# Splitting the list of the halves ahead, loading small slots before the last scatters, and putting the loop of small slots in a branch, in an attention-plus-mixture-of-experts kernel

## The chip, the cores and the metric

One core of a Trainium2 chip runs the whole kernel as one program. The metric is the device time of one execution in microseconds, taken as the median of three runs. The engines are called PE (TensorE, matmuls), DVE (VectorE), ACT (ScalarE), POOL (GpSimd, which also issues the indirect DMAs, that is gathers and scatters by a list of rows) and SP (SyncE, which issues most loads).

## What is computed

Four batches of channel attention are followed by a mixture of experts with one expert for each token (a token is a row of 256 floats; there are 20,224 of them, 8 experts, 1024 hidden features):

```python
qn, kn = q / norm(q, axis=1), k / norm(k, axis=1)
s = kn.transpose(0, 2, 1) @ qn / tau            # 256 x 256 for each batch
x = (v @ softmax(s)).reshape(20224, 256)
out = x
do = x @ w_skip > 0                             # the tokens that are computed
e = argmax(x[do] @ w_gate)                      # one expert each
out[do] += softmax(x[do] @ w_gate)[e] * (relu(x[do] @ w1[e]) @ w2[e])
```

The inputs are drawn from a fixed seed. In them one expert has nearly all of the computed tokens: 9,902, of which 2,461 lie in the first four chunks (below) and 4,941 in the first eight; each of the other seven has at most 54.

## The kernel before

**Phases.** A batch is four chunks of 1,280 tokens, so there are 16 chunks. Step A of a chunk loads q and k and adds to the scores (PE, L731). When a batch's four A steps are done, its softmax runs. Step B of a chunk multiplies v with the softmax (L804 to L806, in two parts of higher and lower bits), ACT copies the rows to `xo` (L811) and stores them to `out`, `logits` and `route` pick an expert for each token, and ten POOL scatters for each chunk (L886) write (token, gate) to the list `lst` in DRAM, where every expert has its own stretch.

**Halves ahead.** While the later B steps run, the kernel already computes experts for the expert with most tokens: nine halves of 512 tokens (H0 to H8), taken from its list as it stands after eight chunks (D0 = 8). After four chunks (D1 = 4) `Large.ahead` picks that expert, so that its weights can be gathered (`w1r`, `w2r`; two POOL gathers). After eight chunks it looks whether the expert has 512·9 + 128 + 64 tokens by then; if so, one POOL load brings their list, `lN`, from `lst`; if not, the address points past the lists, at empty entries. A half then takes four gathers (L213, through `gather_ahead`) into one of three buffers `xg`, eight PE transposes into `pt` (L286), the split of the transposed rows into `xH` (ACT, L288) and `xL` (DVE, L290), two layers of matmuls (L320 to L322 into the buffer `px`, then L342 and L343) and four scatters back to `out` (L218, through `put_ahead`). The weights are split too: `w1H` on ACT (L313), `w1L` on DVE (L315), four pieces each. Before a batch's softmax can be used, the sums of squares `n` (L718, L720) go through PE and DVE (`nrm`, L744), and v is split into `vH` (ACT) and `vL` (DVE, L693).

**Tails.** Steps T0 to T3 compute the first 64 tokens of every expert, two experts at a time (buffers `tg`, weights `v1r` and `v2r`); T4 computes 128 more of the busiest.

**Loops.** What is left of the lists is cut into slots: `large.loop()` (a hardware loop at L447, 1,024 tokens a round; its code for a slot holds L320 x32) and `small.loop()` (L596, slots of 128 tokens). With these inputs the first runs five rounds and the second none. Ahead of the small loop stand its first loads (`load_rows`: five small lists through SP, two gathers into `yg`; `load_weights`: three weight gathers into `v1r` and `v2r`), two transposes and `keep_warm(4)` (four PE products of `ones` that nobody reads). The small loop ends with one scatter, of `yo`.

**What sets the order.** `ORDER` is a string written by hand ("... B9 B2 B3 A10 B4 ... A15 B9 H0 B10 ... H8 T2 T3"); it gives every PE step a nominal time. A list scheduler, `Plan`, gives each task an engine, a cost, the tasks that it depends on and a due time, and writes each engine's instructions in the order that comes out. An engine executes its instructions in that order, so that a waiting instruction holds up those behind it. `now` is the nominal time at the end of the string. At the start of `large.loop()` all engines meet (L447). `beside` and `apart` tell the framework that two groups of transfers don't touch the same data.

## Time and profile before

| | us |
|---|---|
| median of three runs | 800.12 (799.33 to 801.84) |
| the profiled execution | 797.65 |
| its span in the trace | 796.0 |
| PE busy in it | 761.3 (96%) |
| DVE busy | 472.4 (59%) |
| POOL busy | 389.5 (49%) |
| ACT busy | 334.2 (42%) |
| share of the 16 DMA engines: loads, indirect DMAs, stores | 27.3%, 10.5%, 8.2% |

PE is busy nearly all of the time, so a change that doesn't take work from PE can gain at most where PE stands still or runs slowly. The view that finds such places cuts the span into stretches and gives each engine's busy time, and the TensorE clock that was granted (1.00 is the upper of its two levels, 2.4 GHz; 0.50 the lower, 1.2 GHz). The timeline of one engine then lists its instructions with start, duration and, in brackets, the idle time just ahead of an instruction and what ended it.

### The profile page before, as it was taken

To read this page: it belongs to the slowest core of one execution; us is meant where nothing else is said; L and a number is where in the kernel's file an instruction comes from. 1 tells how busy PE (TensorE), PEld (TensorE's weight loads), DVE (VectorE), ACT (ScalarE), POOL (GpSimd) and SP (SyncE) were. 2 spreads that over 40 slices of the span, in tenths; PEclk is the share of its full clock that TensorE was granted. 3 is DMA by queue.
4 is the path that set the end of the run, shared out by engine and by line. 5 is a ranking of instruction groups with operands and counts; after the bars stand their busy time and mean duration, and the time that the engine had idled before them with its cause. 6 is when DMAs were issued, how large, how long until landed. Compare 5 with 4: busy or idle time off the path is not lost. (4 is left out here: it accounts for less than half of the span.)

```text
span 796.0 us, 12212 instructions
## 1 busy us (share of the span) xinstructions
PE 761.3 (96%) x4268; PEld 656.4 (82%) x4268; DVE 472.4 (59%) x968; ACT 334.2 (42%) x515; POOL 389.5 (49%) x411
## 2 busy tenths in 40 slices
PE   6999999999979999999999999996999999999994
PEld 5889998999968989889888886754888888888883
DVE  4809958898978773664547442513555564656652
ACT  5519748668756442432332223112233332423330
POOL 3000277778758777657667523124434344253532
PEclk9999999999998999999999999998999999999997
DMA  8979979899552471641246313453211111111100
GB/s 318 399 251 330 372 247 298 310 396 384 172 184 103 130 219 34 232 147 34 93 163 224 141 41 103 182 217 134 94 46 47 46 47 45 41 47 46 46 20 29
DMA packets 55218, 127.50 MB, mean 160 GB/s; under 512 B 14556, under 2 KB 34792, under 8 KB 52480
## 3 DMA queue, kind: packets, MB, share of 16 engines
q1 hardware_dynamic: 18000, 79.75, 27.3%
q0 software_dynamic: 15936, 26.39, 10.5%
q10 hardware_dynamic: 21232, 20.72, 8.2%
q8 instruction: 27, 0.44, 0.2%
q14 instruction: 23, 0.19, 0.1%
HBM read 109.03 MB, written 31.93 MB: 177 GB/s over the span
## 5 line engine op out<-in xcount | busy, mean ns | idle before, releaser
L886 POOL DMA_INDIRECT lst<-pay,r_posi x160 | 179.5, 1122 | 141.6 <-DVE r_posi L883 93.3
L731 PE MATMUL s<-qt,kt 128*128 128x256 f32 x640 | 150.2, 386 | 6.2 <-DMA kt<-in_k 6.2
L218 POOL DMA_INDIRECT out<-xg,lc x78 | 81.0, 1038 | 142.7 <-DVE xg L349 124.1
L731 PEld LDWEIGHTS s<-qt,kt 128*128 128x128 f32 x640 | 120.1, 193 | 21.0 <-issue 6.2
L342 PE MATMUL po<-w2s,hH 128*128 128x512 f32 x320 | 113.7, 398 | 0.4 <-issue 0.4
L342 PE MATMUL px<-w2s,hH 128*128 128x512 f32 x288 | 102.6, 399 | 0.0
L804 PE MATMUL px<-aH,vH 128*128 128x266 f32 x320 | 99.8, 312 | 0.2 <-ACT xo L811 0.2
L213 POOL DMA_INDIRECT xg<-out,lc x80 | 82.0, 1025 | 31.3 <-issue 18.3
L325 ACT ACTIVATE hH<-ph 128x512 fp32r<-128x512 f32 x80 | 47.9, 599 | 110.4 <-PE ph L322 109.9
L805 PE MATMUL px<-aL,vH 128*128 128x266 f32 x320 | 92.7, 290 | 0.0
L806 PE MATMUL px<-aH,vL 128*128 128x266 f32 x320 | 92.4, 289 | 0.0
L343 PE MATMUL po<-w2s,hL 128*128 128x256 f32 x320 | 89.5, 280 | 0.0
L326 DVE SCALAR_TENSOR_TENSOR hL<-ph,hH 128x512 fp32r<-128x512 f32 x80 | 55.4, 692 | 47.4 <-ACT hH L325 46.4
L343 PE MATMUL px<-w2s,hL 128*128 128x256 f32 x288 | 80.6, 280 | 0.0
L811 ACT COPY xo<-px 128x532 f32<-128x532 f32 x80 | 47.8, 603 | 74.0 <-PE px L806 71.4
L342 PEld LDWEIGHTS po<-w2s,hH 128*128 128x128 f32 x320 | 60.0, 188 | 14.5 <-issue 0.8
L320 PE MATMUL ph<-xH,w1H 128*128 128x512 f32 x160 | 63.4, 396 | 7.0 <-PEq L447 7.0
L416 DVE SCALAR_TENSOR_TENSOR hL<-px,hH 128x512 fp32r<-128x512 f32 x72 | 46.4, 685 | 39.7 <-ACT hH L414 39.6
L342 PEld LDWEIGHTS px<-w2s,hH 128*128 128x128 f32 x288 | 54.0, 188 | 12.7 <-issue 0.8
L321 PE MATMUL ph<-xL,w1H 128*128 128x512 f32 x160 | 63.2, 395 | 0.0
L322 PE MATMUL ph<-xH,w1L 128*128 128x512 f32 x160 | 63.1, 394 | 0.0
L804 PEld LDWEIGHTS px<-aH,vH 128*128 128x128 f32 x320 | 61.5, 192 | 1.7 <-ACT xo L811 0.6
(216 smaller groups left out, 1428.6 us busy)
## 6 DMA issues: line engine op xcount, KB each, us to landing
vf<-in_vt SPq DMA_DIRECT2D x32, 640.0 KB, 7.2
qt<-in_q SPq DMA_DIRECT2D x31, 640.0 KB, 6.5
kt<-in_k SPq DMA_DIRECT2D x31, 640.0 KB, 6.5
out<-xo ACTq DMA_DIRECT2D x12, 1280.0 KB, 7.6
v1r<-in_w SPq DMA_DIRECT2D x8, 1024.0 KB, 6.2
v2r<-in_w SPq DMA_DIRECT2D x8, 1024.0 KB, 4.9
lst<-pay,r_posi POOLq DMA_INDIRECT x160, 4.1
out<-xo ACTq DMA_DIRECT2D x4, 640.0 KB, 6.1
```

Source lines behind the costliest of these rows:

```text
L213: apart(G.indirect_dma_start(out=to, out_offset=None, in_=out[0:n, :], in_offset=IndirectOffsetOnAxis(ap=ls[:, 0:1], axis=0), bounds_check ...
L218: i = (G.indirect_dma_start(out=out, out_offset=IndirectOffsetOnAxis(ap=ls[:, 0:1], axis=0), in_=src, in_offset=None, bounds_check=NTOK - ...
L320: T.matmul(ph, self.w1H[:, fs], self.xH[:, kb, :], start=(kb == 0), stop=False)
L321: T.matmul(ph, self.w1H[:, fs], self.xL[:, kb, :], start=False, stop=False)
L322: T.matmul(ph, self.w1L[:, fs], self.xH[:, kb, :], start=False, stop=(kb == 1))
L342: T.matmul(po, self.hH[:, f, ts], self.w2s[:, f, :, :], start=(f == 0), stop=False, skip_group_check=True)
L343: T.matmul(po[:, :C], self.hL[:, f, ts], self.w2s[:, f, 0, :], start=False, stop=(f == NFB - 1), skip_group_check=True)
L731: T.matmul(sums[b][:, cb, :], kt[:, j % JH, cb * P : (cb + 1) * P], qt[:, j % JH, :], start=(ch == 0 and j == 0 and cb == 0), stop=(ch == ...
L804: T.matmul(px[:, i, :NA], vH[:, kb, js], aH[:, kb, :], start=(kb == 0), stop=False)
L805: T.matmul(px[:, i, :NA], vH[:, kb, js], aL[:, kb, :], start=False, stop=False)
L806: T.matmul(px[:, i, :NA], vL[:, kb, js], aH[:, kb, :], start=False, stop=(kb == 1))
L886: i = G.indirect_dma_start(out=lst, out_offset=IndirectOffsetOnAxis(ap=posi[:, t : t + 1], axis=0), in_=pay[:, t0 + t, :], in_offset=None, ...
```

## The change

1. **The list in two parts.** `lA` (16 columns: halves 0 to 3) is loaded after four chunks, `lB` (21 columns: halves 4 to 8 and T4) after eight. The choice is made twice: at four chunks (at least 512·4 + 64 = 2,112 tokens of one expert, else an address past the lists), and at eight as before. Halves 0 to 3 gather only from the rows of the first four chunks.
2. **Small slots' first loads earlier.** `load_rows` comes in three pieces: the five small lists as soon as the tables are there, the two gathers at a due time of `now` − 6, and the weights (`load_weights`) at `now` − 4 after T2's second layer; before, they had `now` + 6 and `now` + 10, after every scatter of the tails. `keep_warm(12)` stands ahead of `large.loop()`.
3. **The small loop in a branch.** Its transposes, `keep_warm(4)` and the loop are in the `Else` of `tc.If(n < 1)`.

```diff
+KA = 4
-            self.lN = rows([P, 4 * K0 + 1, 2], I32, name="lN")
+            self.lA = rows([P, 4 * KA, 2], I32, name="lA")
+            self.lB = rows([P, 4 * (K0 - KA) + 1, 2], I32, name="lB")
+            self.lN = rows([P, 8, 2], I32, name="lN")
...
+            def address(i, first):
+                V.tensor_scalar(adf, e0, float(CAP), float(E * CAP + first), ALU.mult, ALU.add)
+                V.tensor_scalar(ads[i], adf, float(E * CAP), None, ALU.min)
+
+            V.tensor_reduce(many, cnt4, AX.X, ALU.max)
+            V.scalar_tensor_tensor(most, cnt4, many, iota8, ALU.is_ge, ALU.mult)
+            V.tensor_reduce(top, most, AX.X, ALU.min)
+            V.scalar_tensor_tensor(e0, many, 512.0 * KA + T0, top, ALU.is_ge, ALU.mult)
+            address(0, T0)
...
+            apart(load_list(ads[0], 0, self.lA, 4 * KA, G), "lists A", "of the first chunks alone")
+            yield
...
+            address(1, T0 + 512 * KA)
...
-            beside(load_list(ad0, 0, self.lN, 4 * K0 + 1, G), "first lists", "later lists")
+            apart(load_list(ads[1], 0, self.lB, 4 * (K0 - KA) + 1, G), "lists B", "of the first chunks alone")
...
         def gather_ahead(self, x, t):
             h = self.AHEAD[x]
+            l, y, d = (self.lA, x, D1) if x < KA else (self.lB, x - KA, D0)
             if t == 0:
-                G.tensor_copy(self.lc[h], self.lN[:, 4 * x : 4 * x + 4, :])
-            self.gather_tile(h, t, D0 // NCH * N + D0 % NCH * P * J)
+                G.tensor_copy(self.lc[h], l[:, 4 * y : 4 * y + 4, :])
+            self.gather_tile(h, t, d // NCH * N + d % NCH * P * J)
...
-            if d >= D0:
-                beside(i, "later lists", "first lists")
+            for of, l in ((D1, "lists A"), (D0, "lists B")):
+                if d >= of:
+                    apart(i, l, "of the first chunks alone")
...
-    pick = add("V", 1.5, lambda: next(rows), [based[D1 - 1]])
-    look = add("V", 1.3, lambda: early.append(next(rows)), [based[D0 - 1], pick])
-    lst0 = add("D", 1.0, None, [add("G", 1.05, lambda: next(rows), [look, listed0, stored[D0 - 1]])])
+    pick = add("V", 2.3, lambda: next(rows), [based[D1 - 1]])
+    lstA = add("D", 1.0, None, [add("G", 1.2, lambda: next(rows), [pick, listed4, stored[D1 - 1]])])
+    look = add("V", 1.4, lambda: early.append(next(rows)), [based[D0 - 1], lstA])
+    lstB = add("D", 1.0, None, [add("G", 1.2, lambda: next(rows), [look, listed0, stored[D0 - 1]])])
...
-    sm = add("G", 3.0, lambda: smalls[0].load_rows(slots[0][1], slots[1][1]), [tabled, so, in_order["sc"], *stored.values(), n2, pt], due=now + 6)
-    add("G", 3.2, lambda: smalls[0].load_weights(), [sm, n3], due=now + 10)
...
+    sm = add("V", 1.2, small_rows, [tabled, so, in_order["sc"], *stored.values(), n1])
+    sm = add("D", 1.5, None, [sm])
+    sm = add("G", 3.1, small_rows, [sm, n2], due=now - 6)
+    add("G", 4.0, lambda: smalls[0].load_weights(), [sm, n3, tails[2]], due=now - 4)
...
+        keep_warm(12)
         large.loop()
-        smalls[0].transposed(0)
-        keep_warm(4)
-        smalls[0].loop()
+        with tc.If(smalls[0].n < 1, preferred_fallthrough_block=False) as none_left:
+            pass
+        with none_left.Else():
+            smalls[0].transposed(0)
+            keep_warm(4)
+            smalls[0].loop()
```

**POOL ahead of H0.** POOL's instructions around the first list, before (`lst` are the list's scatters, `xg` the gathers of a half, `lc` the half's own copy of its list):

```order
L225 DMA w1r<-in_w,wc 128x2048
L225 DMA w2r<-in_w,wd 128x2048
L886 DMA lst<-pay,r_posi 168960x2 x40
L230 TENSOR_LOAD ad_2156
L230 ISA x2
L231 ISA
L231 DMA lN<-lst 128x74
L402 COPY lc_152<-lN 128x8
L213 DMA xg_144<-out,lc_152 128x256 x4
L402 COPY lc_153<-lN 128x8
L213 DMA xg_145<-out,lc_153 128x256 x2
```

The same place now:

```order
L226 DMA w1r<-in_w,wc 128x2048
L898 DMA lst<-pay,r_posi 168960x2 x10
L231 TENSOR_LOAD ads_1372
L231 ISA x2
L232 ISA
L232 DMA lA<-lst 128x32
L226 DMA w2r<-in_w,wd 128x2048
L898 DMA lst<-pay,r_posi 168960x2 x20
L412 COPY lc_154<-lA 128x8
L214 DMA xg_144<-out,lc_154 128x256 x4
L412 COPY lc_155<-lA 128x8
L214 DMA xg_145<-out,lc_155 128x256 x4
```

The first list now stands behind 10 scatters that follow `w1r`, not 40, and the gathers of halves 0 and 1 behind 30; the ten scatters of chunk 7 come after ten gathers.

**DVE ahead of H0.** The last instructions of DVE before H0's first matmul (`lg`, `r_mx` and `r_d` are routing), before and now:

```order
L827 COPY lg<-xo 128x100
L744 TENSOR_SCALAR nrm<-n 128x260
L838 TENSOR_REDUCE r_mx<-lg 128x10
L840 TENSOR_TENSOR r_d<-lg,r_mx 128x80
L693 TENSOR_TENSOR vL<-vf,vH 128x1280
L290 TENSOR_TENSOR xL<-pt,xH 128x512
L315 TENSOR_TENSOR w1L<-w1r,w1H 128x512 x4
L290 TENSOR_TENSOR xL<-pt,xH 128x512
```

```order
L756 TENSOR_SCALAR nrm<-n 128x260
L705 TENSOR_TENSOR vL<-vf,vH 128x1280
L318 TENSOR_TENSOR w1L<-w1r,w1H 128x512
L293 TENSOR_TENSOR xL<-pt,xH 128x512
L318 TENSOR_TENSOR w1L<-w1r,w1H 128x512 x3
L293 TENSOR_TENSOR xL<-pt,xH 128x512
L839 COPY lg<-xo 128x100
```

One of the four splits of w1 now stands ahead of the first `xL`, and the routing of the next chunk behind the second. On PE the same products of B stand between the last A and H0 (48 of them), with `n` and the two groups of four transposes spread between them.

**POOL at the entry of the large loop.** Before, and now (`tg` are the tails' scatters; L447, now L457, is the loop):

```order
L218 DMA out<-xg_146,lc_154 20224x256 x4
L218 DMA out<-tg_4566,tl 20224x256
L218 DMA out<-tg_4562,tl 20224x256
L218 DMA out<-tg_4563,tl 20224x256
L218 DMA out<-tg_4564,tl 20224x256
L218 DMA out<-tg_4565,tl 20224x256
L584 MEMSET mc_4558 128x2
L213 DMA yg_4540<-out,mc_4557 128x256
L213 DMA yg_4541<-out,mN_4554 128x256
L225 DMA v1r_4532<-in_w,vc_4549 128x2048
L225 DMA v1r_4533<-in_w,vc_4550 128x2048
L225 DMA v2r_4536<-in_w,vd_4551 128x2048
```

```order
L214 DMA yg_4558<-out,mc_4575 128x256
L214 DMA yg_4559<-out,mN_4572 128x256
L226 DMA w2r<-in_w,wd 128x2048
L219 DMA out<-xg_146,lc_156 20224x256 x4
L219 DMA out<-tg_4584,tl 20224x256
L219 DMA out<-tg_4580,tl 20224x256
L219 DMA out<-tg_4581,tl 20224x256
L226 DMA v1r_4550<-in_w,vc_4567 128x2048
L226 DMA v1r_4551<-in_w,vc_4568 128x2048
L226 DMA v2r_4554<-in_w,vd_4569 128x2048
L219 DMA out<-tg_4582,tl 20224x256
L219 DMA out<-tg_4583,tl 20224x256
```

The two `yg` gathers moved ahead of the scatters of H8, the three weight gathers ahead of the scatters of T2 and T3; behind T3's scatter there is now only the loop.

## Rows read from the trace of the kernel before

**Rows 1.** Busy time by stretch: start and end in us; length; then busy us and count of PE, PEld, DVE, ACT and POOL; the granted clock of PE (1.00 is the upper level); share of the DMA engines; GB/s. The stretches are cut where PE stands still: the last A step ends at 229.34, H0's first matmul starts at 245.54, the last matmul ahead of the large loop ends at 543.22, the clock is back at 554.93, the last matmul of the large loop ends at 783.14.

```profile
6.18:229.34 223.16, 222.68 (x1290) 203.56 (x1291) 171.96 (x322) 150.13 (x183) 101.91 (x87) 1.00 0.88 316
229.34:245.54 16.20, 10.19 (x63) 9.51 (x62) 8.36 (x19) 7.86 (x14) 12.65 (x13) 0.79 0.52 171
245.54:543.22 297.68, 294.58 (x1710) 244.05 (x1708) 156.87 (x382) 95.84 (x176) 167.74 (x169) 1.00 0.40 134
543.22:554.93 11.71, 4.75 (x11) 3.79 (x12) 3.31 (x13) 1.69 (x3) 8.16 (x9) 0.71 0.46 161
...
783.14:796.00 12.86, 1.31 (x11) 1.14 (x10) 0.97 (x2) 0.68 (x2) 2.91 (x3) 0.65 0.10 25
```

**Rows 2.** Timeline of PE, from the last A step (it ends at 229.34) to H0: start us, duration us, instruction, and in brackets the idle time ahead of it and what ended it.

```profile
228.99 0.47 PE L804 MATMUL px<-aH,vH 128*128 128x266 f32 x1
...
232.15 0.59 PE L718 MATMUL n<-sqq,ones 128*128 128x256 f32 x2
...
240.06 0.47 PE L286 MATMUL pt<-ident,xg 128*128 128x128 f32 x1 [3.94 <-DMA xg<-out,lc]
...
245.54 0.39 PE L320 MATMUL px<-xH,w1H 128*128 128x512 f32 x1
```

**Rows 3.** Timeline of POOL from 163 us to 231 us: the first and the last of the 40 scatters of chunks 4 to 7, the list and the first gather of half 0.

```profile
163.18 1.10 POOL L886 DMA_INDIRECT lst<-pay,r_posi  x1 [0.30 <-issue]
...
221.38 1.78 POOL L886 DMA_INDIRECT lst<-pay,r_posi  x1 [0.31 <-issue]
224.92 0.59 POOL L231 DMA_DIRECT2D lN<-lst  x1 [1.76 <-DMA lst<-pay,r_posi]
228.44 0.19 POOL L402 COPY lc<-lN 128x8 int32<-128x8 int32 x1 [2.93 <-DMA lN<-lst]
229.56 1.41 POOL L213 DMA_INDIRECT xg<-out,lc  x1 [0.94 <-POOL lc L402]
```

**Rows 4.** Timelines of DVE and ACT in the same place.

```profile
233.12 0.43 DVE L744 TENSOR_SCALAR nrm<-n 128x260 f32<-128x260 f32 x1
...
233.88 1.53 DVE L693 TENSOR_TENSOR vL<-vf,vH 128x1280 fp32r<-128x1280 f32 x1
241.19 0.69 DVE L290 TENSOR_TENSOR xL<-pt,xH 128x512 fp32r<-128x512 f32 x1 [5.78 <-ACT xH L288]
241.79 2.49 DVE L315 TENSOR_TENSOR w1L<-w1r,w1H 128x512 fp32r<-128x512 f32 x4
...
240.57 0.59 ACT L288 CAST xH<-pt 128x512 fp32r<-128x512 f32 x1 [5.21 <-PE pt L286]
```

**Rows 5.** Timeline of POOL around 330 us (the last gather of half 4) and of PE at 357 us (half 4's transposes).

```profile
331.56 1.00 POOL L213 DMA_INDIRECT xg<-out,lc  x1 [0.30 <-PE px L806]
...
357.02 0.60 PE L286 MATMUL pt<-ident,xg 128*128 128x128 f32 x4
```

**Rows 6.** DMA issues by tile: count and median us from issue to landing.

```profile
xg<-out,lc POOLq DMA_INDIRECT x80, 2.8
out<-xg,lc POOLq DMA_INDIRECT x78, 2.4
v1r<-in_w,vc POOLq DMA_INDIRECT x2, 7.5
```

**Rows 7.** Timeline of PE at the entry of the large loop.

```profile
538.96 3.67 PE L560 MATMUL px<-v2r,thT 128*64 128x256 f32 x32 [0.24 <-ACT thT L552]
542.56 0.66 PE L286 MATMUL pt<-ident,xg 128*128 128x128 f32 x4
550.18 0.76 PE L320 MATMUL ph<-xH,w1H 128*128 128x512 f32 x1 [6.96 <-PEq L447]
...
554.98 0.40 PE L322 MATMUL ph<-xH,w1L 128*128 128x512 f32 x1
555.23 0.40 PE L320 MATMUL ph<-xH,w1H 128*128 128x512 f32 x1
555.46 0.39 PE L321 MATMUL ph<-xL,w1H 128*128 128x512 f32 x1
```

**Rows 8.** Timelines of POOL and of SP's queue ahead of that entry (the row of SP is the two loads of T3's second weights).

```profile
543.44 0.97 POOL L218 DMA_INDIRECT out<-tg,tl  x1 [4.37 <-DVE tg L562]
...
549.14 1.00 POOL L225 DMA_INDIRECT v1r<-in_w,vc  x1 [0.30 <-POOLq L447]
...
528.20 0.80 SPq L514 DMA_DIRECT2D v2r<-in_w  x2
```

**Rows 9.** The instructions of line 447 (the large loop): count, min/median/max ns, first and last start in us. The first start is when that engine's queue reaches the meeting point.

```profile
L447 POOLq EVENT_SEMAPHORE  x82: 17/43/43, 547.6 to 784.2; - x82
...
L447 DVEq EVENT_SEMAPHORE  x68: 21/21/21, 543.9 to 784.3; - x68
```

**Rows 10.** Timeline of all engines from the last matmul of the large loop to the end.

```profile
784.80 1.06 PE L1248 MATMUL m<-ones 128*128 128x128 f32 x8
...
786.43 0.97 POOL L218 DMA_INDIRECT out<-xg,lc  x1 [0.30 <-POOLq L596]
792.31 0.97 POOL L218 DMA_INDIRECT out<-yo,mc  x1 [4.90 <-PEq L1298]
```

**Rows 11.** The jumps of line 596 (the small loop, which runs no round): count, min/median/max ns, first and last start.

```profile
L596 ACTq COMPARE_BRANCH  x2: 34/36/38, 786.4 to 786.5; - x2
L596 PEldq COMPARE_BRANCH  x2: 69/2068/4067, 786.5 to 786.7; - x2
```

More of the change, by code (lines that the diff above doesn't have):

```diff
@@ L370, in ahead @@
         def ahead(self, cnt0, cnt4):
-            top = tab.tile([P, 1], F32, name="top")
-            V.tensor_reduce(top, cnt4, AX.X, ALU.max)
-            V.scalar_tensor_tensor(cnt4, cnt4, top, iota8, ALU.is_ge, ALU.mult)
-            V.tensor_reduce(top, cnt4, AX.X, ALU.min)
-            most = tab.tile([P, E], F32, name="most")
-            V.tensor_scalar(most, iota8, top, None, ALU.is_equal)
+            top, many, e0, adf = (tab.tile([P, 1], F32, name=n) for n in ("top", "many", "e0", "adf"))
+            ads = [tab.tile([P, 1], I32, name=f"ads{i}") for i in range(2)]
+            most, start = (tab.tile([P, E], F32, name=n) for n in ("most", "start"))
+            def address(i, first):
[6 more added lines that the diff above has]
+            address(0, T0)
+            V.tensor_scalar(start, iota8, e0, 512.0 * KA, ALU.is_equal, ALU.mult)
+            V.tensor_scalar(start, start, float(T0), None, ALU.add)
+            V.tensor_scalar(most, iota8, e0, None, ALU.is_equal)
             V.tensor_scalar(top, top, float(E), None, ALU.add)
@@ L1075, in attn_moe @@
             listed0 = add("D", 0.06, None, [in_order["sc"]])
+        if d == D1 - 1:
+            listed4 = add("D", 0.06, None, [in_order["sc"]])
         if d == NC - 1:
@@ L1128, in attn_moe @@
         for i in range(4):
-            gt = then("gat", add("G", 1.31 if i else 1.9, lambda x=x, i=i: large.gather_ahead(x, i), [lst0, puts.get(x - 3)]))
+            gt = then("gat", add("G", 1.31 if i else 1.9, lambda x=x, i=i: large.gather_ahead(x, i), [lstA if x < KA else lstB, puts.get(x - 3)]))
             gd = add("D", 0.36, None, [gt])
@@ L1199, in attn_moe @@
         tw = [None] * 4 if p == NP else [then("tw", add("D", 2.95, small("tail_weights", p, w, u), [so, (firsts, tails)[w].get(p - 2)], nominal["T", p, 2 * w] - 1)) for w in range(2) for u in range(2)]
-        tg = then("tg", add("G", 1.3, small("tail_gather", p), [tld, listed0 if p == NP else None]))
+        tg = then("tg", add("G", 1.3, small("tail_gather", p), [tld, lstB if p == NP else None]))
         tgd = add("D", 0.3, None, [tg])
@@ L1235, in attn_moe, with small_rows @@
     n3.deps.append(tails[NP])
[L1236 to L1237 removed]
+    def small_rows():
+        if not early[2:]:
+            early.append(smalls[0].load_rows(slots[0][1], slots[1][1]))
+        next(early[2])
+    sm = add("V", 1.2, small_rows, [tabled, so, in_order["sc"], *stored.values(), n1])
+    sm = add("D", 1.5, None, [sm])
+    sm = add("G", 3.1, small_rows, [sm, n2], due=now - 6)
+    add("G", 4.0, lambda: smalls[0].load_weights(), [sm, n3, tails[2]], due=now - 4)
     def counts():
```

17 lines of the change are left out of this document (6 added, 11 removed).

## Prediction

> **What bounds the kernel now.** I read the busy time by stretch first [rows 1]. PE works through the A steps without a gap (222.68 us busy of 223.16) and nearly so from H0 to the large loop (294.58 of 297.68); the change takes no matmul out of these. What it can win lies in three stretches where PE stands still and then, or meanwhile, runs at a lower granted clock: 16.20 us ahead of H0 (10.19 busy, clock 0.79), 11.71 us at the entry of the large loop (4.75 busy, clock 0.71), and 12.86 us from the last matmul to the end (1.31 busy). Each of the three parts of the change aims at one of them, so I read the timelines of the engines there.
>
> Ahead of H0, PE is ready to transpose and waits for gathers: the last wait is 3.94 us, for xg [rows 2]. Behind that wait stands POOL: it issues the 40 scatters of chunks 4 to 7 from 163.18 to 223.16, waits 1.76 us for the last one to land, loads the list, waits 2.93 us for that, and starts the first gather at 229.56, after the last A step [rows 3]. POOL's place in its own queue is the bound.
>
> At the loop's entry PE's last work starts at 542.56 and takes 0.66, so it ends at 543.22; the first product of the loop starts at 550.18, released by the meeting of the engines [rows 7]. DVE reaches the meeting at 543.9, POOL only at 547.6 [rows 9]: after T3's scatter (543.44, 0.97 us) it still issues the first loads of the small slots, the last but one at 549.14 [rows 8]. After the pause the products start too far apart until about 555: 11 of them take 4.80 us (550.18 to 554.98), at 0.23 us each afterwards they would take 2.5 [rows 7].
>
> At the end, POOL's scatters of the last slot start by 786.43, but one more, of yo, from a loop that runs no round, starts only at 792.31 [rows 10]. It waits for PE's jump past that loop's code: 4.07 us for PE, 0.04 for ACT [rows 11].
>
> **Part 1, the list.** Forty scatters took 59.98 us, 1.50 each [rows 3]. The first list now stands behind ten of them and the gathers of halves 0 and 1 behind twenty more, one list load (0.59 and up to 2 of waiting, which the next weight gather covers) and w2r. So the scatters of chunk 6 end near 163 + 30·1.5 = 208; eight gathers at 1.31 (1.00 and 0.31 between) end near 219, and land 2.8 us later by the median [rows 6]. Even at three times that landing they are there before PE ends the A steps at 229.34. The wait for xg goes.
>
> What is late next? PE has the same work left after the last A: 48 products of B from 228.99 on (24 of them took 3.16 us, so 6.32), n and its pair (232.15 to 233.12, when DVE takes it over: 0.97) and two groups of transposes (0.66 each): 228.99 + 6.32 + 0.97 + 1.32 = 237.6 [rows 2, 4, 7]. DVE's row, as now ordered: n is ready one group of 12 products earlier, so near 231.6, plus nrm, vL (0.43 and 1.53, with what stands between them: 2.3 from nrm's start to vL's end), one w1L (0.62), xL (0.69, for which pt and the 0.59 of xH are ready by then), three w1L (1.87) and the second xL (0.69): 231.7 + 2.3 + 0.6 + 0.7 + 1.9 + 0.7 = 237.9, and 0.2 for the handing over [rows 4]. So H0 starts near 238.1, DVE just behind PE, against 245.54: **7.4 us**. Since PE no longer pauses for long, its clock should not fall there either; that is in the 237.6, which uses full-clock durations.
>
> Costs: some five more DVE operations on 8 numbers (0.2 us each) in a phase in which DVE works 171.96 of 223.16 us: nothing, unless DVE is behind there. Ten gathers of 128 KB go from the quiet stretch (DMA share 0.52) to one with share 0.88 at 316 GB/s [rows 1]: 1.3 MB, up to 4.1 us of transfers ahead of the q and k loads. I take 0 to 1 of it, since POOL's scatters go down at the same time and PE had no wait for a load worth naming there. The order of A and B steps changes too, as the scheduler's times shift from 152 us on; I take 0.4 for both, so **7.0**, with bounds of 4 (half of the wait comes back as other waits) and 8.5. The ten scatters of chunk 7 move behind ten gathers (13 us) and so does everything that waits for lB; half 4, its first user, had its last gather at 331.56 and its transposes at 357.02 [rows 5], 24 us of cover.
>
> **Part 2, the loop's entry.** Behind T3's scatter POOL has nothing left, so it reaches the meeting near 543.44 + 0.97 = 544.4 and not 547.6 [rows 8, 9]; DVE is at 543.9 there. The meeting let PE start 1.1 us after POOL's passing (549.1 to 550.18) [rows 7, 8], so PE could go at 545.6. keep_warm(12) stands ahead of it: four such products show as eight rows in 1.06 us [rows 10], so twelve take 3.2, from 543.2 to 546.4. The first product of the loop then starts at 546.45: 3.7 us earlier, and without a pause, so at full clock: 4.80 − 2.5 = 2.3 us more. I take **6.1**. If keep_warm doesn't hold the clock, 3.7 is left; if the meeting stays later for another engine, 3; without keep_warm in the way it would be 6.5.
>
> What it costs: three weight gathers of 1 MB now run while T3 computes, and POOL issues them ahead of T2's and T3's scatters (3 × 1.31 = 3.9 us); they wait for T2's second layer, which is over when T3's starts at 538.96 [rows 7], so they are out by 542.9, ahead of T3's scatter. The small lists now stand ahead of loads of the tails in SP's queue, but are issued when their tables are there, long before. Nothing else of it lies on the path.
>
> **Part 3, the branch.** With no round to run, PE jumps over the small loop's code straight after the large loop, and the yo scatter is not issued. What ends last is then the last scatter of the large loop (786.43 + 2.4 to landing = 788.8) or PE's jump, if it takes the same 4.07 us: from 784.4, when the engines leave the large loop, to 788.5. From the issue of yo's scatter the span took 3.69 us to its end (792.31 to 796.0); the same from 786.43 gives 790.1. I add 0.3 for the jump, which may end last: 790.4, so **5.6 us** [rows 1, 6, 9 to 11]. Bounds: 6 if the jump is done first, 1.5 if a second such jump follows on it (5.6 − 4.07).
>
> A rule speaks against this part. In the rows, one of PE's two jumps took 4,067 ns and the other 69, those of ACT 34 to 38 [rows 11]: a far jump on the engine with the most code is dear, a near one is not. The Trainium skill, in "Runtime: NRT & Kernel Launch", section "Instruction fetch mechanics", says that a taken branch whose target is outside the window of fetched instructions has to wait for its target to be fetched, and counts that among the reasons why control flow at run time is expensive. By that rule the added branch adds a wait of its own; the rows agree that PE pays it, but it pays it already for the loop that the branch now encloses.
>
> **The sum.** 7.0 + 6.1 + 5.6 = 18.7 us. On the profiled execution (797.65, span 796.0) that gives 779.0; that execution was 2.5 us under the median, and the median of 800.12 becomes 781.4.
>
> **The rivals.**
>
> *B. Another wait takes the place of xg's ahead of H0.* DVE and ACT have to make xH, xL, w1H, w1L and vL in one row there, and ACT's order changed as well. For it: by the sum above DVE is already the last by some 0.5 us, so any slip of DVE costs its whole length. Against it: its work there is 6 us in all. It would halve part 1: 800.12 − (3.5 + 6.1 + 5.6) = 784.9.
>
> *C. The entry stays bound.* For it: the weight gathers landed 7.5 us after issue [rows 6], and they now run beside the loads of T3's second weights (issued at 528.20, needed at 538.96) and ahead of two scatters. If T3 or its scatter slips by three or four microseconds, or the clock falls all the same, part 2 keeps 2.5: 800.12 − (7.0 + 2.5 + 5.6) = 785.0. Against it: the v2r load has some 10 us from issue to use, and the gathers start hardly before that use.
>
> *D. A second dear jump at the end.* PE jumps to the branch's end and from there on; if both cost 4.07 us, or the jump starts only when POOL's scatters are done, part 3 keeps 1.5: 800.12 − (7.0 + 6.1 + 1.5) = 785.5. For it: the 4.07 in the rows; against it: the second jump there took 0.07. The Trainium skill's rule above would have it this way if the code after the branch lies outside what is fetched.
>
> *E. Slower: the first list is empty.* The choice at four chunks wants 2,112 tokens of one expert; with fewer, lA points past the lists, halves 0 to 3 compute on nothing, and 2,048 tokens go to the large loop, two more rounds. Five rounds took 550.18 to 783.14, 46.6 us each [rows 1, 7]: 781.4 + 93 = 874. It decides at 2,112, and these inputs have 2,461 by then, so it takes an error in the counting of chunks.
>
> **How the numbers follow.** Forecast 0.64, B 0.15, C 0.10, D 0.09, E 0.02. The range: down to 777.5 with every gain at its upper bound (8.5 + 6.5 + 6 = 21, 779.1) and the spread of the runs of before (799.33 is 0.8 under the median); up to 788 for one rival together with the lower end of another part's mid-range (800.12 − 12). B, C and D alone lie inside it, so what is left out is E and pairs of rivals, some 0.15. About 0.3% (2.4 us) is what a measurement can tell from no change. All cases but E are faster by more than that; for two or three rivals at once with an added wait I leave 0.02: faster 0.96, same 0.02, slower 0.02.
>
> **What would show it.** Right: gathers of halves 0 and 1 on POOL well before the last A step; no idle of PE ended by xg ahead of H0, and H0 within 9 us of the last A; a clock of 1.00 in that stretch and at the loop's entry; less than 1 us of PE idle between keep_warm and the loop; no scatter of yo, and the end 7 to 8 us after the last matmul. Wrong: PE waits there for xH, xL, vL or w1L (B); POOL again last at the meeting, or slow products after it (C); a jump of PE that starts after 786 or two of 4 us (D); seven rounds of the large loop (E). The prediction fails most easily in part 1, where the half microsecond between DVE and PE is worked out from durations that a different order may change.

## The result, and the profile after

| | before | changed |
|---|---|---|
| median us (four runs each) | 799.73 (798.0 to 801.84) | 776.38 (776.02 to 778.65) |
| profiled execution, us | 797.65 | 776.19 |
| its span | 796.0 | 774.6 |
| granted clock of PE over the span | 0.986 | 0.998 |

The changed kernel takes 0.9713 of the time before (95% interval 0.9683 to 0.9743): faster by 23 us, where 18.7 were forecast, and its median lies below the range. In three of the five jobs with experiments every kernel, the one before too, was slow (medians 834 to 856 us), so the times of those jobs are set aside and not compared with others.

The busy time by stretch of the changed kernel. The cuts are those of [rows 1], but for the fourth stretch: no clock falls there now, so it is cut at the first second layer of the loop, where [rows 1] cuts at the clock's return (after the first column: length; then busy us and count of PE, PEld, DVE, ACT, POOL; granted clock; DMA share; GB/s):

```profile
6.53:228.02 221.49, 221.18 (x1290) 202.62 (x1291) 172.23 (x319) 150.15 (x183) 106.95 (x90) 1.00 0.90 323
228.02:235.78 7.76, 7.76 (x63) 7.55 (x62) 6.26 (x14) 5.59 (x11) 6.24 (x6) 1.00 0.34 101
235.78:534.50 298.72, 294.43 (x1710) 244.38 (x1709) 160.22 (x402) 98.17 (x180) 179.75 (x181) 1.00 0.43 147
534.50:548.23 13.73, 13.73 (x75) 11.77 (x74) 8.12 (x15) 6.81 (x12) 6.43 (x8) 1.00 0.16 53
548.23:767.47 219.24, 219.24 (x1153) 187.66 (x1151) 123.80 (x216) 72.94 (x129) 87.90 (x94) 1.00 0.14 43
767.47:774.60 7.13, 0.00 (x0) 0.00 (x0) 0.97 (x2) 0.00 (x0) 1.95 (x2) 0.78 0.15 45
```

Ahead of H0 and at the loop's entry PE is now busy in all of the stretch, at full clock; ahead of the last product only the third line shows more than 0.4 us of idle time (294.43 busy of 298.72). Where the 21.4 us of the two profiles come from is read off by the starts of the same matmuls in both (an A product is a product of step A, `s<-qt,kt`):

| from the start of, to the start of | before | changed | difference |
|---|---|---|---|
| span to the last A product | 228.96 | 227.64 | −1.32 |
| last A to H0 | 16.58 | 8.14 | −8.44 |
| H0 to the last transposes ahead of the loop | 297.41 | 298.61 | +1.20 |
| these to the loop's first product | 7.23 | 2.87 | −4.36 |
| first product to the first second layer (L342, now L345) | 13.79 | 10.97 | −2.82 |
| this to the last product | 218.89 | 218.96 | +0.07 |
| last product to the end | 13.09 | 7.38 | −5.71 |

More than half of the first row is there before the two kernels differ in PE's order (from 150.9 us on). The same product at 120 us, before and after:

```profile
120.19 0.27 PE L861 MATMUL m<-r_rc,tri_r 128*128 128x8 f32 x1 [0.28 <-DVE nrm L744]
...
119.45 0.27 PE L873 MATMUL m<-r_rc,tri_r 128*128 128x8 f32 x1 [0.29 <-DVE nrm L756]
```

**Ahead of H0.** POOL's timeline after (the load of lA, half 0's first gather, half 1's last), then PE's and DVE's, which answer to [rows 2 to 4]:

```profile
175.02 0.61 POOL L232 DMA_DIRECT2D lA<-lst  x1
...
209.19 2.02 POOL L214 DMA_INDIRECT xg<-out,lc  x1 [0.27 <-POOL lc L412]
...
222.52 1.25 POOL L214 DMA_INDIRECT xg<-out,lc  x1 [0.30 <-issue]
```

```profile
231.74 0.60 PE L289 MATMUL pt<-ident,xg 128*128 128x128 f32 x4
...
233.79 0.66 PE L289 MATMUL pt<-ident,xg 128*128 128x128 f32 x4
...
235.78 0.40 PE L323 MATMUL px<-xH,w1H 128*128 128x512 f32 x1
```

```profile
230.67 1.48 DVE L705 TENSOR_TENSOR vL<-vf,vH 128x1280 fp32r<-128x1280 f32 x1
232.07 0.68 DVE L318 TENSOR_TENSOR w1L<-w1r,w1H 128x512 fp32r<-128x512 f32 x1
233.04 0.69 DVE L293 TENSOR_TENSOR xL<-pt,xH 128x512 fp32r<-128x512 f32 x1 [0.29 <-ACT xH L291]
...
235.45 0.68 DVE L293 TENSOR_TENSOR xL<-pt,xH 128x512 fp32r<-128x512 f32 x1
```

The gathers of halves 0 and 1 are out by 223.8, and no transpose waits. H0 starts at 235.78, while DVE is still at the second xL (235.45 to 236.13): by the kernel, H0's first three products need only the first piece, and the fourth starts at 236.48, so PE doesn't wait for DVE.

**A new wait.** Half 3's gathers (POOL) and its transposes (PE):

```profile
306.90 1.07 POOL L214 DMA_INDIRECT xg<-out,lc  x1 [0.27 <-POOL lc L412]
...
311.73 0.99 POOL L214 DMA_INDIRECT xg<-out,lc  x1 [0.30 <-issue]
...
315.65 0.55 PE L289 MATMUL pt<-ident,xg 128*128 128x128 f32 x3
317.95 0.33 PE L289 MATMUL pt<-ident,xg 128*128 128x128 f32 x1 [1.75 <-DMA xg<-out,lc]
```

PE comes to half 3 some ten microseconds earlier than before (315.65, before 325.77); its gathers stand behind the scatters of half 0 and twenty scatters of the list, and the last one lands 1.75 us late: PE can go on 6.2 us after its issue, where the median from issue to landing is 2.8. This wait is 1.75 of the 4.29 us of idle time in the third line above; the rest is no more than what stood in this stretch before (3.10 us in [rows 1]).

**The loop's entry and the end,** which answer to [rows 7 to 11]: PE's timeline, the instructions of the loop's line (first start: when that queue reaches the meeting), POOL's last scatter, and the jumps of the new branch:

```profile
534.01 0.66 PE L289 MATMUL pt<-ident,xg 128*128 128x128 f32 x4
534.50 2.84 PE L1271 MATMUL m<-ones 128*128 128x128 f32 x24
537.26 0.47 PE L323 MATMUL ph<-xH,w1H 128*128 128x512 f32 x1
```

```profile
L457 POOLq EVENT_SEMAPHORE  x82: 17/43/43, 534.7 to 768.6; - x82
L457 ACTq EVENT_SEMAPHORE  x68: 17/17/17, 534.8 to 768.6; - x68
L457 PEldq EVENT_SEMAPHORE  x68: 51/51/51, 535.2 to 768.6; - x68
L457 DVEq EVENT_SEMAPHORE  x68: 21/21/21, 535.5 to 768.6; - x68
```

```profile
770.76 0.97 POOL L219 DMA_INDIRECT out<-xg,lc  x1 [0.30 <-DMA out<-tg,tl]
```

```profile
L1286 PEldq COMPARE_BRANCH  x1: 4215/4215/4215, 768.8 to 768.8; - x1
...
L1286 POOLq COMPARE_BRANCH  x1: 58/58/58, 769.9 to 769.9; - x1
```

POOL is no longer the last at the meeting, DVE is, and PE has no pause. (Two of the weight gathers of the small slots now land 10.5 us after their issue, before 7.5 [rows 6], but nothing on the path waits for them.) At the end PE jumps from 768.8 to 773.0, beside POOL's last scatter, which is issued at 770.76 and ends the kernel.

### The profile page after: what moved, and what is told of

Its sections match the earlier page's. It is cut to its first block, busy times and chain, and to the rows that moved or that the text cites. A ratio compares the mean times of both kernels' runs of the same rounds, so it can differ in the third digit from the quotient of the medians.

```text
span 774.6 us, 12180 instructions
## 1 busy us (share of the span) xinstructions
PE 756.3 (98%) x4282; PEld 654.0 (84%) x4282; DVE 472.8 (61%) x972; ACT 333.7 (43%) x513; POOL 394.5 (51%) x411
## 5 line engine op out<-in xcount | busy, mean ns | idle before, releaser
L898 POOL DMA_INDIRECT lst<-pay,r_posi x160 | 181.6, 1135 | 138.1 <-DVE r_posi L895 90.6
L743 PEld LDWEIGHTS s<-qt,kt 128*128 128x128 f32 x640 | 119.3, 192 | 21.1 <-issue 6.5
L345 PE MATMUL po<-w2s,hH 128*128 128x512 f32 x320 | 113.7, 397 | 0.0
L214 POOL DMA_INDIRECT xg<-out,lc x80 | 87.7, 1097 | 29.3 <-issue 17.7
L345 PE MATMUL px<-w2s,hH 128*128 128x512 f32 x288 | 102.6, 398 | 0.0
L345 PEld LDWEIGHTS po<-w2s,hH 128*128 128x128 f32 x320 | 60.0, 188 | 13.6
L345 PEld LDWEIGHTS px<-w2s,hH 128*128 128x128 f32 x288 | 54.0, 188 | 12.5 <-issue 0.8
L424 ACT ACTIVATE hH<-px 128x512 fp32r<-128x512 f32 x72 | 39.8, 598 | 51.3 <-PE px L325 50.0
```

Source lines behind the costliest of these rows:

```text
L214: apart(G.indirect_dma_start(out=to, out_offset=None, in_=out[0:n, :], in_offset=IndirectOffsetOnAxis(ap=ls[:, 0:1], axis=0), bounds_check ...
L345: T.matmul(po, self.hH[:, f, ts], self.w2s[:, f, :, :], start=(f == 0), stop=False, skip_group_check=True)
L743: T.matmul(sums[b][:, cb, :], kt[:, j % JH, cb * P : (cb + 1) * P], qt[:, j % JH, :], start=(ch == 0 and j == 0 and cb == 0), stop=(ch == ...
L898: i = G.indirect_dma_start(out=lst, out_offset=IndirectOffsetOnAxis(ap=posi[:, t : t + 1], axis=0), in_=pay[:, t0 + t, :], in_offset=None, ...
```

## Experiments

The first job took the kernel before once more and each part alone (its hunks of the diff, nothing else).

**The kernel before, again.**

> The kernel before, unchanged, for the span and the granted clock of each of its runs. Theory (the sum of the three stages): the profiled execution had gone 21.4 us down (span 796.0 to 774.6), the median 23.4; the 2 us between the two are runs of before in which the clock was low for longer than in the profiled one: spans from 796 to 800 with clocks from 0.986 down to about 0.980, each 0.001 of clock worth some 0.8 us. Rival (loads): the spans differ by the first q and k loads, at one and the same clock of 0.986.

Measured: 797.62 us (792.85 to 804.6, twelve runs), ratio 1.0009 (0.9977 to 1.0041). Spans from 791.2 to 802.9, clocks from 0.988 down to 0.982: the scatter belongs to the kernel, and the longer runs are mostly those with less clock. The clock isn't all of it: by the expectation's 0.8 us for each 0.001 it gives some 5 us, and the spans differ by 11.7. Its profile shows another run of the same order: PE waits for aT, the copy that the softmax's last product needs, and the clock falls behind that wait; PE, ACT, and the busy time by stretch:

```profile
200.63 1.74 PE L780 MATMUL m<-w,aT 128*128 128x10 f32 x8 [3.24 <-ACT aT L775]
```

```profile
197.36 0.57 ACTq L822 DMA_DIRECT2D out<-xo  x1
...
198.68 0.27 ACT L843 ACTIVATE r_ex<-r_d 128x80 f32<-128x80 f32 x1 [4.25 <-issue]
```

```profile
190.00:200.80 10.80, 7.56 (x44) 6.51 (x42) 5.59 (x16) 6.31 (x12) 8.20 (x9) 1.00 0.72 258
200.80:207.70 6.90, 6.90 (x22) 5.91 (x23) 4.44 (x13) 4.10 (x6) 5.53 (x4) 0.51 0.95 206
```

The last A step then comes at 234.4, the gathers are no longer late for it, and H0 starts at 244.15, not 245.54. PE's jump at the end took 1,205 ns in this run, so that the end came 10.1 us after the last product and not 13.1:

```profile
L596 PEldq COMPARE_BRANCH  x2: 69/637/1205, 786.3 to 786.4; - x2
```

**Part 1 alone.**

```diff
-            self.lN = rows([P, 4 * K0 + 1, 2], I32, name="lN")
+            self.lA = rows([P, 4 * KA, 2], I32, name="lA")
+            self.lB = rows([P, 4 * (K0 - KA) + 1, 2], I32, name="lB")
...
```

> Part 1 alone (list in two parts). Sum theory: 7 to 9 us under before (stage ahead of H0 8.4 us shorter, 1.9 us of it given back by half 3's rows), H0 within 8 us of the last A step, PE idle of 1.5 to 2 us ahead of half 3's transposes; loop entry and end as before. Rival (chance of the first loads): 1.3 us of the gain lie ahead of the last A step and don't come back here, so 6 to 7.

Measured: 787.36 us (785.24 to 790.09) beside 797.57 of before, ratio 0.9852 (0.9814 to 0.9889): 10.2 us by the medians, 11.8 (8.9 to 14.8) by the ratio, the medians' more than either theory had. From the last A to H0 8.13 us; half 3's wait is there (1.99 us), and the clock fell behind it (0.50 from 319.6 to 323.1), so that H0 to the last transposes took 300.4 us.

**Part 2 alone.**

```diff
+    sm = add("G", 3.1, small_rows, [sm, n2], due=now - 6)
+    add("G", 4.0, lambda: smalls[0].load_weights(), [sm, n3, tails[2]], due=now - 4)
...
+        keep_warm(12)
```

> Part 2 alone (small loads ahead of the last scatters, keep_warm(12)). Sum theory: 6.5 to 7.5 us under before: 4.4 from an earlier first product of the loop, 2.3 from the clock, 0.4 from the wait ahead of the first second-layer product. Rival (the loads collide without part 1's earlier halves): 3 to 5.

Measured: 792.31 us (789.31 to 796.16), ratio 0.9908 (0.9874 to 0.9942): 5.3 us by the medians, 7.3 (4.6 to 10.0) by the ratio, so it can't choose between the theories; the profile does. 2.94 us from the last transposes to the loop, 10.98 from there to the second layer, as in the changed kernel (7.1 us less than before). In this profile the late list hit half 1 (waits of 1.47 and 2.95 us for xg at 257 to 261, and a low clock behind), a third place of the same loss.

**Part 3 alone.**

```diff
+        with tc.If(smalls[0].n < 1, preferred_fallthrough_block=False) as none_left:
+            pass
+        with none_left.Else():
...
```

> Part 3 alone (the small loop in a branch). Sum theory: 5.5 to 6 us under before, nothing of it ahead of the last matmul; PE's one jump of about 4.2 us starts as the large loop is left. Rival (the jump is dear and counts): 2 us or less.

Measured: 792.99 us (789.94 to 800.2), ratio 0.9941 (0.9911 to 0.9971): 4.6 us by the medians, 4.7 (2.3 to 7.1) by the ratio. 7.40 us from the last product to the end; the jump takes 4.39 us from 786.1 on and is hidden. As the end of before takes 10.1 to 13.1 us (its jump 1.2 to 4.1), the gain is 2.7 to 5.7 by the run. The three parts' ratios add up to 3.0% (20.1 us by the medians), the whole is 2.9%: within the intervals of 0.3 to 0.4% of each part, they neither help nor hinder each other.

The next four went together, in a job in which before took 844.99 us.

**The changed kernel, again.**

> The changed kernel, unchanged, beside the next three on the same chip. It should lie at 775.5 to 777.5 with runs within 3 us of each other, and the span of a run should follow its granted clock: 0.998 near 774.5, 0.995 near 777.

Measured: 844.53 us, ratio to before 0.9987 (0.9955 to 1.002), clocks from 0.957 to 0.969. Nothing of the gain shows in the times of this job. Its profile shows where the time goes: PE stands still within a half's products, ended by nothing that the profile shows, and the low clock comes behind these pauses (PE, then the busy time by stretch):

```profile
323.66 0.28 PE L346 MATMUL px<-w2s,hL 128*128 128x256 f32 x1 [1.02 <-issue]
...
328.58 0.37 PE L346 MATMUL px<-w2s,hL 128*128 128x256 f32 x1 [1.70 <-issue]
```

```profile
322.00:328.00 6.00, 2.38 (x9) 1.36 (x8) 0.00 (x0) 0.00 (x0) 4.48 (x6) 1.00 0.02 1
328.00:341.70 13.70, 7.80 (x20) 5.31 (x20) 2.44 (x5) 0.58 (x1) 7.70 (x9) 0.50 0.15 44
```

In all ten profiles of the three jobs set aside, PE's pauses of 0.15 us and more between 20 us and the loop add up to 34 to 47 us, against 3 to 12 in the ten others. From the last transposes on, the changed kernel takes what it takes elsewhere: 2.87, 11.0, 218.96 and 7.36 us. So the stages of parts 2 and 3 are as short here as there; why PE pauses ahead of the loop, and whether before does so too (no trace of it in these jobs), stays open; most landings of DMAs are missing from these profiles, so a wait for one isn't excluded.

**Half 3's gathers due earlier.**

```diff
-            gt = then("gat", add("G", 1.31 if i else 1.9, lambda x=x, i=i: large.gather_ahead(x, i), [lstA if x < KA else lstB, puts.get(x - 3)]))
+            gt = then("gat", add("G", 1.31 if i else 1.9, lambda x=x, i=i: large.gather_ahead(x, i), [lstA if x < KA else lstB, puts.get(x - 3)], nominal["H", 1, 4] if x == 3 else 1e9))
```

> The changed kernel, with half 3's four gathers due earlier: six of the twenty scatters of the list that stood ahead of them now stand between and behind them. Theory: PE's wait of 1.8 us ahead of half 3's transposes goes (and with it the low clock that followed it in part 1 alone, 319.6 to 323.1), so 1.5 to 2.5 us under the changed kernel, and no run at clock 0.995. Rival: the six scatters reach the list later and put off a later half, so no gain.

Measured: 845.64 us, runs from 827.96 to 851.98, too far apart for so small a question; measured again below.

**Without keep_warm(12).**

```diff
-        keep_warm(12)
         large.loop()
```

> The changed kernel without keep_warm(12) ahead of the large loop. Theory (the pause, not its cause, costs the clock): the first product of the loop comes at most 0.5 us earlier after the last transposes, since the engines' meeting takes about as long as the twelve products; PE stands still for about 2.5 us, and if the clock falls after that, the products until it is back cost 2 us or more: 1.5 to 2.5 us slower than the changed kernel. Rival (the pause is too short to matter): 0 to 0.5 us faster.

Measured: 836.0 us, not comparable; but the entry can be read: 2.87 us from the last transposes to the first product, as with the twelve products, then 3.4 us of low clock (589.9 to 593.3), and 12.6 us to the second layer against 11.0.

**Without the small loop and its branch** (it leaves out the loop of small slots, which runs no round here).

```diff
-        with tc.If(smalls[0].n < 1, preferred_fallthrough_block=False) as none_left:
...
```

> The changed kernel with the small loop and its branch left out altogether (these inputs have no small slot; the loads for it stay): what the branch itself still costs. Theory (the last scatter's landing ends the kernel, PE's jump of 4.2 us is hidden beside it): 0 to 0.6 us faster than the changed kernel. Rival (the jump is the last): 1 us or more faster.

Measured: 836.23 us, not comparable; 7.36 us from the last product to the end, and as much with the branch in the same job. The branch costs nothing there.

In the third job before took 797.2 us again (seventeen runs).

**The store behind aT, in the kernel before.**

```diff
-        st = then("st", add("S", 0.06, lambda d=d: store(d), [s], nominal["B", d, 4] + 3))
+        st = then("st", add("S", 0.06, lambda d=d: store(d), [s, ready_a[2, "aT"] if d == 7 else None], nominal["B", d, 4] + 3))
```

> The kernel before, with one move on ACT and no other instruction displaced: the two stores of chunk 7 stand behind the softmax's aT of the third batch, not ahead of it. Theory (the part of the gain that the forecast lacked is this store: it waits for the store before it to land, up to 21 us under load, and aT, and with it PE, waits behind it): 1.5 to 4 us under before in the median, the wait of PE ahead of the product of w and aT gone (0.5 to 3.2 us in four profiles of this order), no low clock near 200 us, and the runs of before above 800 us gone. Rival (before's scatter has another cause): same median and same spread of 8 to 10 us.

Measured: 795.85 us (794.14 to 800.16), ratio 0.9983 (0.9959 to 1.0007): not told from no change. The runs spread over 6.0 us (before 7.9), and one of twelve is above 800 us (before five of seventeen). The wait for aT is gone in the profile, and H0 starts at 245.33, as in the first profile of before. The expectation of 1.5 to 4 us fell: as long as the gathers set H0, a wait ahead of them is covered by them.

**The changed kernel, half 3's gathers early, and no keep_warm,** in the same job.

> The changed kernel, unchanged, beside the other three. If the chip grants the clock as for its first four runs: 775.5 to 777.5, 21 to 23 us under before.

> The changed kernel with half 3's gathers due earlier, again, since the runs on the second chip were under a low clock throughout. Theory: PE's wait of 1.8 us ahead of half 3's transposes is gone, 1.5 to 2.5 us under the changed kernel. Rival: another half waits instead, no gain.

> The changed kernel without keep_warm(12), again. From the profile on the second chip: the loop's first product comes no earlier without it (2.87 us after the last transposes start, as with it), and the products after it ran at the lower clock for 3.4 us, so 1.5 to 2 us slower than the changed kernel. Rival: on a chip that grants more clock the pause of 2.6 us is harmless, 0 to 0.3 us of difference.

Measured: changed 776.1 us (774.12 to 778.2), ratio 0.9724 (0.9693 to 0.9756); half 3's gathers early 774.42 us (773.99 to 775.09), 0.970 (0.9669 to 0.9731); no keep_warm 776.81 us (775.85 to 779.86), 0.973 (0.9697 to 0.9763). With the gathers earlier half 3's transposes stand without a wait, the runs lie within 1.1 us of each other (4.1 before this edit), and five of the changed kernel's six runs lie above all of them: this version is the fastest, by 1.7 us in the median (the intervals of the two ratios overlap). The changed kernel's own profile in this job had no wait at half 3 either: there the last gather was issued at 309.43 and not 311.73, and that run is the fastest of its six (774.12). Half 3 with its gathers early (POOL's last gather, PE), and then half 3's last transpose in the profile without keep_warm, with the clock behind it:

```profile
308.87 1.04 POOL L214 DMA_INDIRECT xg<-out,lc  x1 [0.30 <-PE px L818]
...
315.36 0.66 PE L289 MATMUL pt<-ident,xg 128*128 128x128 f32 x4
```

```profile
318.54 0.33 PE L289 MATMUL pt<-ident,xg 128*128 128x128 f32 x1 [1.77 <-DMA xg<-out,lc]
```

```profile
312.00:318.70 6.70, 4.93 (x26) 3.98 (x24) 5.07 (x17) 3.19 (x6) 5.28 (x4) 1.00 0.97 307
318.70:322.20 3.50, 3.50 (x18) 3.50 (x18) 2.64 (x7) 1.69 (x3) 0.97 (x1) 0.51 1.06 401
```

The wait of 1.8 us is followed by a low clock here, and the same wait was not in the changed kernel's first profile: H0 to the last transposes takes 296.8 us without the wait, 298.6 with it, 300.2 to 300.4 with the clock fallen. Without keep_warm, PE at the loop's entry:

```profile
539.29 0.47 PE L323 MATMUL ph<-xH,w1H 128*128 128x512 f32 x1 [2.64 <-issue]
...
540.87 0.63 PE L323 MATMUL ph<-xH,w1H 128*128 128x512 f32 x1
```

The first product comes 2.91 us after the last transposes start; behind the pause the clock falls (540.6 to 544.0) and the stretch to the second layer takes 12.6 us, not 11.0. In three of its six runs the clock over the whole span stayed at 0.998, as in the changed kernel's first profile, where it fell nowhere ahead of the end (this profile has 0.994), so it seems not to fall there; in the median the twelve products are worth 0.7 us, which isn't told apart.

**The list in two parts with the old order of A and B.** The scheduler's due times are kept as in the kernel before, so that PE's and ACT's instructions up to H0 stand as there; then the same with the store behind aT. Both went twice beside the changed kernel.

```diff
-        before = [(d, t) for t in self.tasks for d in t.deps]
+        before = [(d, t) for t in self.tasks for d in t.deps if not (id(d), id(t)) in self.unheard] + self.heard
...
+    plan.unheard.update((id(d), id(gA)) for d in gA.deps)
...
+                plan.heard.append((lstB, gt))
```

> The changed kernel with all three parts, but with the steps of A and B on PE and everything on ACT up to the halves in the order of before (the scheduler's due times there are those of before); the list is still in two parts, and half 0's gathers still end before the last A step. Theory (two bounds in a row: behind the late gathers stands a store that makes aT, and PE, wait, and only the new order takes that away too): last A step at 230 to 234 in the profile and low clock near 200 us in most runs, H0 some 8 us after it, so 2 to 4 us slower than the changed kernel, and runs 4 us and more apart. Rival (the order is worth nothing, as moving the store alone suggested): within 1 us of the changed kernel.

> The same as the kernel with the old order, with one move more: the two stores of chunk 7 behind aT on ACT. Theory of two bounds: PE's wait ahead of the product of w and aT is gone, the last A step at 228 to 229, and the time falls back to within 1 us of the changed kernel. Rival: no difference from the old order with the store in its place.

> Again the three parts with the old order of A, B and ACT, since the last job ran under a low clock throughout. Theory of two bounds, as before, with one number more from the profile under the low clock: from the last A step to H0 9.7 us, not 8.1 (DVE's old order, routing ahead of the splits); so 1.6 us for that and up to 4 for the store's wait, 2 to 4 us slower than the changed kernel. Rival: within 1 us of it.

> The same with the store's move. Theory of two bounds: 1 to 2 us slower than the changed kernel (the 9.7 us stay), and no wait of PE ahead of the product of w and aT. Rival: as the kernel with the old order.

> The changed kernel, unchanged, beside the two with the old order: 775.5 to 777 if the chip grants the clock as for its first runs.

> The changed kernel, unchanged, for the comparison within the job: 775.5 to 777 if the chip grants the clock as for its first runs.

Measured: both jobs are among those set aside (before 856.34 and 845.58 us). Medians 848.53, 848.82 and the changed kernel 853.44 in the first, 834.37, 834.13 and 839.14 in the second, with runs up to 29 us apart: they tell nothing of a few microseconds, and the changed kernel's gain over before is nothing in the first (ratio 0.9999) and 0.9% in the second. From the last A product to H0, a stretch at full clock in all of these profiles, they say more: 9.73, 9.90, 9.75 and 9.75 us in the old order, with the gathers in time; 8.2 to 9.8 us in the six profiles of the new order in the jobs set aside, the longer ones with pauses ended by nothing that the profile shows. The two other jobs make it plain: 9.75 us in both profiles of the old order in which half 0's gathers came in time (the kernel before, again, and part 2 alone), 8.13 or 8.14 in all five of the new order. In the old order PE waits twice there, the second time for DVE's vL (PE's timeline, list in two parts with the old order, second job):

```profile
245.75 0.63 PE L289 MATMUL pt<-ident,xg 128*128 128x128 f32 x4 [0.57 <-issue]
...
247.52 0.39 PE L818 MATMUL px<-aH,vL 128*128 128x266 f32 x1 [0.90 <-DVE vL L705]
```

So 1.6 of the 8.4 us from the last A to H0 is the new order, and the rest the list. The order also goes with the wait for aT: 2.3 to 3.2 us of it in three of the four profiles from the other jobs that have the old order and the store in its place, none in the five that have the new. What that is worth in the median, once the list is early, stays open.

## Why the prediction was wrong

The mechanisms were right at all three places, and B, C, D and E did not come; the size was 5.0 us short (776.4 against 781.4). Two steps failed: the step to the median, for 2.3 us of it, and the sizes of the terms, for 2.7 (21.4 between the profiles against 18.7).

**The step from the profiled execution to the median** (the profiled one "was 2.5 us under the median, and the median of 800.12 becomes 781.4") carried an offset over as if it belonged to any kernel. It is where one run happens to lie among others: the profiled run of before lay 2.5 and then 3.3 us under its median, that of the changed kernel 0.2 and then 2.0. With half 3's gathers early all runs lie within 1.1 us. Before, runs lie up to 12 us apart, and its profiles show why: H0 starts anywhere from 243.4 to 247.8, as the waits fall on half 0, on half 1 or on aT; PE's jump takes 1.2 to 4.1 us; and behind the pauses the clock is low for 3.4 to 10.2 us. Three runs were also few for a base: in the two later jobs at full clock before took 797.57 and 797.2 us (24 and 17 runs), against which the sum of 18.7 gives 778.5 to 778.9. The low end of the range came from the same base and failed with it; its own working, 779.1 less 0.8, gives 778.3, not the 777.5 that stands there. That the base was high and the offset large in those few runs is luck. The changed kernel gains 21.1 us in the job with seventeen runs of before, and 21.4 between the profiles.

**The terms.** Part 1, taken at 7.0, measured 8.6 between the two profiles (1.32 + 8.44 − 1.20; 7.8 without the luck in the first of these, see below), and 10.2 us alone by the medians. Its wait for xg went as forecast, gathers out by 223.8 (forecast: near 219). Three things were mis-sized:
- H0 was to start 9.1 us after the last A product and started 8.1 after it. The sum gave each group of four transposes 0.66 us, the row's modelled length, while the next product starts 0.36 to 0.41 after the group does; and it made H0 wait for DVE's second xL, which the first products don't need. DVE was not the last, so the half microsecond added for it fell away, and the transposes took another half less.
- The new order of A and B was priced at a small cost and is a gain: 1.6 us ahead of H0, shown by the old order with gathers in time. The price was set without comparing which wait each order leaves on PE. Of the 1.3 us ahead of the last A step, 0.7 are luck and not the change's, as the product at 120 us shows: it comes at 119.0 to 120.7 in the five profiles of the new order from the jobs at full clock. From that product to the last A it is 108.8 us before, and 108.2 both in the changed kernel and in part 1 alone, so the order gives some 0.6 there. From that product to H0 the five profiles of the new order from the jobs at full clock take 116.3 or 116.4 us, the five of the old one 122.8 to 127.9, the shortest of them with 4.4 us of waits at half 1 afterwards.
- Half 3 had no term. The forecast gave half 4 a cover of 24 us and took it for the first at risk; half 3's gathers, behind twenty scatters in the new order and needed ten microseconds earlier, were late by 1.8 to 2.0 us in three of the four profiles from the jobs at full clock that have the gathers in that place, and in time in one. Moving them takes 1.7 us off the median.

Part 2, taken at 6.1, measured 7.2: the engines' meeting and the twelve products overlap more than the sum had it (2.87 us from the last transposes, forecast 3.5 on the same count), and the 0.41 us of idle time ahead of the second layer went too, 2.8 for the stretch to it in place of 2.3. (Its own terms, 3.7 and 2.3, add up to 6.0.) That keep_warm holds the clock is shown by leaving it out, in both profiles without it; that it stands in the way of nothing too: the first product comes at the same distance without it.

Part 3, taken at 5.6, measured 5.7 between the profiles, and 4.7 (2.3 to 7.1) by the ratio of part 3 alone, since the jump that it hides is short in some runs. The jump of the branch took 4.1 to 4.4 us on PE in the five profiles from the jobs at full clock that have it, 0.06 on POOL; in the jobs set aside it took 3.9 to 4.3 in eight profiles and 0.47 in one. The Trainium skill says in "Runtime: NRT & Kernel Launch", section "Instruction fetch mechanics", that a taken branch out of the fetched window has to wait for its target to be fetched; the long jumps agree with that, but no trace shows what PE waited for. The jump is hidden, as forecast, beside POOL's last scatters, and leaving the branch out gains nothing (7.36 us to the end either way).

## What to carry to other kernels

Work from pauses out: a kernel whose engine pauses can scatter by more than the pauses' length (here by 12 us, and by 1.1 once most were gone), because the pauses fall in different places and the clock falls behind some of them and not others, so a change that removes pauses should be reckoned against many runs of before, not against one profile and its distance from a small median. When work in a queue moves forward, go through every user of that queue in the new order, the one with the least cover first: the consumers come earlier too. And take the length of a step in a chain from start to start of what follows it, not from the duration that its row gives.

## What the runs showed of the hardware

- A wait of 1.8 to 2.0 us at one and the same place was followed by a low clock in two profiles (319.6 to 323.1, 318.7 to 322.2) and by none in a third. Behind a pause of 2.6 us at the loop's entry it fell in both profiles that have it; the clock of other runs' whole spans suggests that it doesn't always.
- PE's jump past the same code of the small loop took 1.21, 1.26, 1.60, 4.07 and 4.09 us in five profiles in which it stood on the path; its jump past the branch around that code took 3.9 to 4.4 us in thirteen profiles and 0.47 in one.
- A store of 1.28 MB from ACT landed 5.8 to 6.4 us after its issue at some places of the kernel before, and 16 to 21 us after it at others, in the stretch with a DMA share of 0.9 (176.1 to 197.3 in its second profile).
- In the three jobs set aside the mean clock of PE was 0.950 to 0.976, and the low clock goes with pauses of PE: in the profile of the changed kernel in the first of them PE pauses from 322.6 us on at full clock, and the clock falls at 328.0. Most of these pauses lie within runs of products and are ended by nothing that the profile shows; in the hardware loop there are none (218.96 us from its first second layer to the last product in all ten profiles, as elsewhere). Before took 797.2 us in one job and 856.34 in a later one on the same chip number, so it isn't the chip alone. The changed kernel gained nothing in two of these jobs (844.53 against 844.99 us, ratio 0.9999) and 0.9% in the third.
